# A two-stage attention and expert kernel: a greedy planner's order replaced by a written-out table of steps

## The chip, the cores and the metric

The kernel runs on one core of a Trainium2 chip. The metric is the device time of one execution in microseconds. The kernel before took 181.87 us in the median of three runs, which lay between 181.1 and 185.36 us.

## The reference

The input x has 4 batches of 10048 rows with 128 columns; `inducing` has 32 rows. The first part is attention in two steps, the second a mixture of 16 experts in 4 groups:

```python
def mab(q, kv):
    s = scale * (q @ kv.transpose(0, 2, 1))
    s = s - s.max(-1, keepdims=True)
    a = np.exp(s)
    a /= a.sum(-1, keepdims=True) + 1e-09
    return a @ kv
h = mab(I, x)            # 32 means of each batch
x2 = mab(x, h)           # each row: a mixture of its batch's 32 means
# mixture of experts, for each row of x2:
g_idx = np.argmax(x2 @ w_group); g_w = softmax(...)[g_idx]
e_idx = np.argmax(x2 @ w_expert[g_idx]); e_w = softmax(...)[e_idx]
out = g_w * e_w * (np.maximum(x2 @ w1[g_idx, e_idx], 0) @ w2[g_idx, e_idx])
```

Each row of x2 is a weighted sum of only 32 means. The fast path works out one expert for a batch from the sum of its means, checks afterwards that all its rows chose that expert and that no hidden unit changes its sign, and then needs the expert only for the means: a matrix G of 32 rows for each batch, so that a row of the output is its 32 attention weights times G. Where a check fails, a general path (behind a branch at the end) computes the batch again. With these inputs it isn't taken.

## The kernel before, in words

Each batch is cut into 5 chunks of 4 x 512 rows, named (b, k). x comes transposed, 1 MB a chunk, into a ring of ten tiles xk; for 11 of the 20 chunks the untransposed rows come too (xm, a ring of two), for the other 9 TensorE turns them (`turn`, L356, copied to xn).

First pass, `chunk`: scores of the 32 inducing rows (L392), their maxima on VectorE (L394 to L399), exp on ScalarE (L402, L405), TensorE turns the result (L410, copied to pt), and weighted sums of the rows are added up in hacc (L428, L434, L436). `common` (L443 to L459) brings the four row groups of a batch to one maximum and gives a factor fc. `mean` (L468 to L485) multiplies the sums of weights by fc, adds them over the four groups with a matmul against same_m (L471), inverts, scales hacc, and a second matmul (L482) gives hT, the means.

`routes` (L501 to L524): two matmuls of the means with the routing weights, then VectorE works out the index of the expert, pi (L505 to L517), and the routing rows own, rd and rbd (L520 to L524). `expert` reads pi into a register of SyncE (L531) and loads that expert's w1 and w2, 512 KB each (L532, L533). From these come G: L537, L547, L565, L575 on TensorE, with copies and VectorE steps in between.

Second pass, `att2`: scores against the means (L597), VectorE turns them (L602) and takes maxima (L606), GpSimd subtracts (L608), ScalarE takes exp (L610), the tile is turned (by TensorE, L644, or VectorE, L653), multiplied with the routing rows (L618), copied and turned again (L629). `gates` does a group of one to three chunks at once (L669 to L695) and gives a weight per row. `outputs`: GpSimd multiplies by it (L725), the tile is turned, four matmuls with G into two double PSUM banks (L743), two copies on ScalarE or VectorE, and the store of 1 MB (L749). All copies go through one helper, L323. `checks`, `bounds` and `verdict` prove the fast path.

All DMAs, loads and stores, are issued by SyncE, in order. So is every other engine's work: the helper `in_order` ties each instruction to the one before it on its engine.

What that order is comes from a planner at build time. Each of these functions is a generator that yields where it changes its engine. `Pace` follows the instructions written so far with a price for each kind and says when each engine and tile is free. `Plan.step` takes, among the jobs that may go on, those that start soonest, and of these the one with the least key (batch and chunk, with offsets such as LAG, and from 60 us on a list MOVES of single offsets). Loads are written when a tile of their ring is free (`load`). The helper `sooner` picks ScalarE or VectorE for a copy, `either` GpSimd or VectorE for a product. Where the planner sees TensorE idle for 0.75 us, `fill` writes matmuls of ones (L276) which nobody reads.

Of the kernel before, what the change touches and what calls it, by code (L numbers as in the profile page):

```python
# [8 lines left out]
F32 = mybir.dt.float32  # L9
# [36 lines left out]
BY_PE = {(B - 2, 0),(B-2, 1)} | {(B - 1, g) for g in range(3)}  # L46
TURNED = [(B - 1, NK - 1)]
FROM = 60.0
MOVES = {("att2", 0, 0): 0.97, ("att2", 0, 3): -1.54, ("att2", 0, 4): 0.83, ("att2", 1, 1): -1.59, ("att2", 1, 2): 0.72, ("att2", 2, 0): 2.99, ("att2", 2, 1): -1.6, ("att2", 3, 3): -0.39, ("checks", 0, 0): -0.44, ("checks", 0, 1): -0.21, ("checks", 1, 0): -1.76, ("checks", 2, 0): -0.25, ("checks", 2, 1): 1.39, ("checks", 3, 1): -0.16, ("chunk", 0, 0): -0.34, ("chunk", 0, 1): 2.5, ("chunk", 1, 3): -0.99, ("chunk", 2, 2): 1.06, ("chunk", 2, 3): 0.44, ("chunk", 3, 1): -0.47, ("chunk", 3, 2): -0.09, ("common", 0): 2.12, ("common", 2): 0.29, ("common", 3): -0.14, ("gates", 1, 0): -1.63, ("gates", 3, 0): -0.76, ("gates", 3, 2): 4.14, ("mean", 3): -3.64, ("outputs", 0, 0): -1.99, ("outputs", 0, 1): -1.63, ("outputs", 0, 3): 1.67, ("outputs", 1, 1): -0.98, ("outputs", 1, 2): -1.75, ("outputs", 2, 2): 1.19, ("outputs", 2, 3): 0.02, ("outputs", 3, 0): -1.03, ("outputs", 3, 4): -0.19, ("routes", 0): 1.12, ("turn", 0, 0, 0): 0.41, ("turn", 0, 0, 1): 1.96, ("turn", 0, 1, 1): -1.1, ("turn", 0, 3, 0): 0.09, ("turn", 2, 1, 0): -2.53, ("turn", 2, 3, 1): 0.09, ("turn", 3, 1, 0): 1.12, ("turn", 3, 3, 0): -1.91}
SIDES = {("at", 0, 0): 0, ("at", 0, 1): 1, ("at", 2, 1): 0, ("et", 0, 0): 0, ("et", 1, 2): 0, ("et", 3, 0): 0, ("out", 0, 4, 0): 0, ("out", 1, 0, 0): 0, ("out", 1, 1, 0): 0, ("out", 2, 1, 0): 0, ("out", 2, 2, 1): 0}  # L50
IDLE = 0.75
THIRD = 2.5
SECOND = -0.2
SWAP = 0.5
SPARE = 1.0
PAIRS = 2
LAG = 5

CHUNKS = [(b, k) for b in range(B) for k in range(NK)]
# [1166 lines left out]
```

## Time and profile before

| | |
|---|---|
| median of 3 runs | 181.87 us (181.1 to 185.36) |
| the profiled execution | 182.77 us, its span 180.9 us |
| mean granted TensorE clock | 0.983 |
| busy: PE, DVE, ACT, POOL | 158.7, 112.4, 111.7, 57.9 us |
| moved by DMA | 57.94 MB, 37.00 read from HBM, 20.58 written |
| expert loads issued, batches 0 to 3 | 37.7, 75.6, 113.8, 138.6 us |
| first and last store issued | 67.2, 173.8 us |

PE is TensorE, DVE VectorE, ACT ScalarE, POOL GpSimd, SP SyncE; PEld is TensorE's load of weights. A float32 matmul appears as two records of PE, a transpose as one. A group's line gives the source line, engine, operation, output and inputs, count, busy time in us and mean duration of one in ns, then the idle time of the engine just before, and what ended it. A line of the timeline or of the chain starts with the start in us and the duration in us; "x8" at its end is the number of records merged. Busy time is the union, so that records that overlap count once.

### The profile page before, as it was taken

The page shows a single profiled execution, that of the slowest core. Times are in us where ns is not written, and L with a number is a line of the kernel's source. Part 1 is how long each engine was busy: PE and PEld are TensorE (multiplying, and loading weights), DVE is VectorE, ACT ScalarE, POOL GpSimd, SP SyncE. Part 2 cuts the span into 40 slices and gives each one's busy share as a digit, 9 for nine tenths or more (in the row PEclk, how much of TensorE's full clock was granted, in tenths as well). Part 3 has the DMA queues.
Part 4 walks back from the last instruction along what each step waited for, and adds up shares of the span by engine and source line. Part 5 has one row for each costly group of instructions (what it writes and reads, how often), then busy time and mean ns, then how long its engine had stood idle before and what let it go on. Part 6 is the DMA issues. An engine that isn't in the chain of part 4 may idle for free.

```text
span 180.9 us, 4715 instructions
## 1 busy us (share of the span) xinstructions
PE 158.7 (88%) x1839; PEld 89.9 (50%) x1839; DVE 112.4 (62%) x334; ACT 111.7 (62%) x198; POOL 57.9 (32%) x85
## 2 busy tenths in 40 slices
PE   2998979998897999999989999989989889899910
PEld 1365746564573644543667446447753346456400
DVE  0143146479589882995897797775868856765300
ACT  3086744852467578558877399577448577756640
POOL 1000000024141943143217470152291934574000
PEclk9999999999999999999999999999999999999985
DMA  4999999999999578999999999895004996609791
GB/s 117 354 429 428 411 426 409 427 408 384 402 423 415 172 239 297 422 418 395 393 413 418 395 372 426 324 359 202 0 0 199 278 421 266 208 6 406 313 368 67
DMA packets 14524, 57.94 MB, mean 320 GB/s; under 512 B 1312, under 2 KB 7584, under 8 KB 8608
## 3 DMA queue, kind: packets, MB, share of 16 engines
q1 hardware_dynamic: 14496, 57.58, 81.9%
q8 instruction: 16, 0.26, 0.6%
q14 instruction: 12, 0.10, 0.1%
HBM read 37.00 MB, written 20.58 MB: 318 GB/s over the span
## 4 chain that ended last, share of the span: by engine, by line
PE 48%; DMA 32%; DVE 5%; ACT 5%; issue 3%; SPq 3%; ACTq 0%; DVEq 0%
DMA xk<-xT 16%; PE pp L743 10%; DMA xm<-xm 9%; PE ps L428 7%; DMA w1s<-w 7%; PE ps L597 5%; PE pp L356 4%; PE ps L392 4%; PE ps L644 4%; PE ps L276 3%; ACT osb L323 3%; PE ps L618 2%; PE ps L410 2%; PE ps L629 2%; PE ps L547 1%
## 5 line engine op out<-in xcount | busy, mean ns | idle before, releaser
L323 ACT COPY osb<-pp 128x1024 f32<-128x1024 f32 x40 | 39.1, 1020 | 18.7 <-PE pp L743 14.3
L608 POOL TENSOR_TENSOR e<-e,mxe 128x512 f32<-128x512 f32 x20 | 20.8, 1048 | 71.4 <-DVE mxe L606 70.3
L725 POOL TENSOR_TENSOR e<-e,w 128x512 f32<-128x512 f32 x20 | 20.6, 1048 | 26.4 <-ACT w L323 14.9
L743 PE MATMUL pp<-et,G 32*128 32x512 f32 x160 | 25.9, 640 | 0.1
L323 ACT COPY xn<-pp 128x1024 f32<-128x1024 f32 x18 | 18.1, 1018 | 9.0 <-PE pp L356 8.9
L394 DVE TENSOR_REDUCE mx<-ps 128x1 f32<-128x512 f32 (+1 forms) x20 | 13.5, 675 | 15.0 <-PE ps L392 14.7
L392 PE MATMUL ps<-xk,indT_sb 128*32 128x512 f32 (+1 forms) x144 | 18.6, 592 | 1.1 <-DMA xk<-xT 1.1
L597 PE MATMUL ps<-xk,hT 128*32 128x512 f32 x144 | 18.1, 598 | 0.6 <-ACT et L323 0.6
L602 DVE STREAM_TRANSPOSE e<-ps 128x512 f32<-128x512 f32 x20 | 14.0, 704 | 5.3 <-PE ps L597 4.3
L402 ACT ACTIVATE pe<-ps,nb 128x512 f32<-128x512 f32 (+1 forms) x20 | 13.8, 689 | 5.6 <-DVE nb L399 3.0
L323 ACT COPY pt<-ps 128x512 f32<-128x512 f32 (+2 forms) x24 | 11.8, 525 | 8.3 <-PE ps L410 8.1
L356 PE MATMUL pp<-cst,xk 128*128 128x128 f32 x128 | 16.5, 276 | 0.3 <-DMA xk<-xT 0.3
L356 PEld LDWEIGHTS pp<-cst,xk 128*128 128x128 f32 x128 | 14.0, 141 | 3.6 <-issue 1.4
L653 DVE STREAM_TRANSPOSE et<-e 128x512 f32<-128x512 f32 x21 | 14.2, 694 | 1.4 <-POOL e L725 1.4
L610 ACT ACTIVATE e<-e 128x512 f32<-128x512 f32 x20 | 12.3, 636 | 4.3 <-POOL e L608 4.3
L606 DVE TENSOR_REDUCE mxe<-e 128x16 f32<-128x512 f32 x20 | 13.5, 677 | 0.4
L743 PEld LDWEIGHTS pp<-et,G 32*128 32x128 f32 x160 | 7.9, 182 | 10.4 <-ACT osb L323 5.8
L428 PE MATMUL ps<-xm,pt 128*32 128x129 f32 (+1 forms) x352 | 11.9, 275 | 1.0 <-DVE hacc L436 0.5
L410 PE MATMUL ps<-cst,pe 128*128 128x128 f32 x80 | 12.4, 282 | 0.3 <-ACT w L323 0.3
L410 PEld LDWEIGHTS ps<-cst,pe 128*128 128x128 f32 x80 | 8.7, 142 | 5.4 <-ACT cr L405 1.6
L428 PEld LDWEIGHTS ps<-xm,pt 128*32 128x32 f32 (+1 forms) x352 | 9.3, 110 | 4.0 <-issue 1.7
L644 PE MATMUL ps<-cst,e 128*128 128x128 f32 x76 | 11.0, 280 | 0.0
(130 smaller groups left out, 229.1 us busy)
## 6 DMA issues: line engine op xcount, KB each, us to landing
xk<-xT SPq DMA_DIRECT2D x18, 1024.0 KB, 13.3
out<-osb SPq DMA_DIRECT2D x16, 1024.0 KB, 7.0
xm<-xm SPq DMA_DIRECT2D x11, 1032.0 KB, 12.4
out<-osb SPq DMA_DIRECT2D x3, 928.0 KB, 7.8
w1s<-w SPq DMA_DIRECT2D x4, 512.0 KB, 7.4
w2s<-w SPq DMA_DIRECT2D x4, 512.0 KB, 8.4
x<-xT SPq DMA_DIRECT2D x4, 256.0 KB, 3.8
x<-xT SPq DMA_DIRECT2D x1, 1024.0 KB, 8.4
```

The costliest lines, as they stand in the source:

```text
L323: (nc.scalar.copy if engine == ACT else nc.vector.tensor_copy)(out=out, in_=in_)
L356: nc.tensor.transpose(ps[:tw, (i * J + j) * P:(i * J + j + 1) * P], xks[b, k][:, j, at:at + tw], ident)
L392: nc.tensor.matmul(ps[32 * j:32 * j + 32, :w], lhsT=indT_sb, rhs=xks[b, k][:, j, off:], start=True, stop=True)
L410: nc.tensor.transpose(ps[:tw, t * P:(t + 1) * P], pe[:, t * P:t * P + tw], ident)
L428: nc.tensor.matmul(hq[32 * j:32 * j + 32, 0:C + 1], lhsT=pt[:tw, t, 32 * j:32 * j + 32], rhs=xn[:tw, t, j, :], start=(t == 0), stop=(t == ...
L597: nc.tensor.matmul(ps[32 * j:32 * j + 32, :], lhsT=hTs[b][:, 0:M], rhs=xks[b, k][:, j, :], start=True, stop=True)
L602: nc.vector.transpose(out=e.rearrange("p t m -> p (t m)"), in_=ps)
L608: either().tensor_tensor(out=e, in0=e, in1=mx[:, :, None].broadcast_to([P, TQ, M]), op=ALU.subtract)
L644: nc.tensor.transpose(ps[:, t * P:(t + 1) * P], e[:, t * J:(t + 1) * J, :].rearrange("p q m -> p (q m)"), ident)
L653: nc.vector.transpose(out=et, in_=e.rearrange("p t m -> p (t m)"))
L725: either().tensor_tensor(out=e, in0=e, in1=w[:, i * T:(i + 1) * T, None].broadcast_to([P, T, M]), op=ALU.mult)
L743: nc.tensor.matmul(pss[j // n][:, j % n * KW:(j % n + 1) * KW], lhsT=Gs[b][32 * j:32 * j + 32, :], rhs=rows, start=True, stop=True)
```

## The change

The planner goes: `Pace`, `Plan`, `Job`, the keys and offsets. In its place stands a table, ORDER, of 701 words. Each word is one step of one job: a letter for the kind, then batch and chunk (or group). The kernel goes through the words and lets the named generator run to its next yield. A second list, ON_DVE, names the copies and products that go to VectorE; all others go to ScalarE or GpSimd.

The letters: x, n loads; t turn; c chunk; h common; m mean; r routes; e expert; a att2; g gates; u outputs; k checks; q the ratios that were the end of `expert`; b bounds; v verdict; f a fill.

```python
for name in ORDER.split():
    job = (name[0], *map(int, name[1:]))
    if job not in jobs:
        jobs[job] = kinds[name[0]](*job[1:])
    next(jobs[job])
in_order(tc, begin)
```

The table begins, and goes on around the last batch's expert, and ends, with these words:

```
x01 f f f f f f f f f f f c00 t00 t00 t00 t00 f t01 c00 c00 c01 x02 c00 c00 x03 t01 t01 t01 x04 n02 c02 x10 n04 c01 c02 x11 x12 c00 c00 c03 c02 c02
...
m3 m3 e2 e2 a24 a24 u10 u21 u21 r3 r3 e3 e2 e2 u10 u10 u10 u10 a23 a24 g21 g21 a33 u20 u20 u20 u21 u21 u21 u21 a33 a33 a33 a33 r3 k21 a30 a30 a30 a30
a32 a32 a32 a32 g21 u20 u20 u22 u22 a33 a33 e3 a31 a31 a33 a33 a34 a30 u20 u22 a34 u20 a31 e3 e3 a32 a32 k21 u22 u23 u23 u23 a32 a32 a32 u24 e3 e3 u22
u23 u22 a32 a33 g31 q2 a31 a31 u23 u23 u23 a30 a30 u24 u24 a31 a31 e3 e3 g31 a30 u24 u24 e3 a31 a31 a30 a30 a31 u24 u24 u14 u14 u14 g31 u33 a34 a34
g30 g30 a34 e3 u14 u33 u33 f f u33 u33 u33 u33 g30 u32 u32 u32 q2 a34 a34 u32 u32 u32 u32 q0 u31 u31 u31 u30 u30 u30 a34 a34 a34 q3 q3 u31 u31 k30 k31
g32 g32 g32 u34 u34 k32 q1 q1 u31 u31 k32 f f u30 u30 u30 u30 f f f u34 u34 u34 u34 u34 q0 f f b b f f b b v f v v
```

Beside the order, the steps between a batch's last sum and its expert's loads are other ones. `common` sends the maximum to all groups with four matmuls and no copy, and multiplies fc into a copy of same_m; `mean` has one step of matmuls and one of VectorE:

```diff
-            nc.vector.tensor_tensor(out=ssum, in0=ssum, in1=fc, op=ALU.mult)
-            nc.tensor.matmul(tot_ps[:, 0:1], lhsT=same_m, rhs=ssum, start=True, stop=True)
-            nc.vector.tensor_scalar_add(rin, tot_ps[:, 0:1], EPS)
-            nc.vector.reciprocal(out=rin, in_=rin)
-            nc.vector.tensor_tensor(out=rin, in0=rin, in1=fc, op=ALU.mult)
-            nc.vector.tensor_scalar_mul(hqs, hacc[:, 0:C], rin)
-            nc.tensor.matmul(hT_ps[:, 0:P + 1], lhsT=hqs, rhs=same_m1, start=True, stop=True)
-            nc.vector.tensor_copy(out=hT4, in_=hT_ps[:, 0:P + 1])
...
+        nc.vector.tensor_scalar_mul(tl([P, P], f"samec{b % 2}"), same_m, fc)
...
+        nc.tensor.matmul(ps[:, P:P + M], lhsT=hacc[:, C:C + 1].broadcast_to([P, P]), rhs=sc[:, 0:M], start=True, stop=False)
+        nc.tensor.matmul(ps[:, P:P + M], lhsT=ones[0:1, 0:P], rhs=eps[:, 0:M], start=False, stop=True)
+        nc.tensor.matmul(ps[:, 0:P], lhsT=hacc[:, 0:C], rhs=sc, start=True, stop=True)
+        yield
+        nc.vector.reciprocal(out=rin, in_=ps[:, P:P + M])
+        nc.vector.tensor_tensor(out=hT4[:, 0:P].rearrange("p (j m) -> p j m", j=J), in0=ps[:, 0:P].rearrange("p (j m) -> p j m", j=J),
+                                in1=rin[:, None, :].broadcast_to([P, J, M]), op=ALU.mult)
+        nc.vector.reduce_sum(out=hT4[:, P:P + 1], in_=hT4[:, 0:M], axis=AX.X)
```

`routes` gives the index in one reduction, as a step of its own ahead of own, rd and rbd; the load of the register no longer checks its bounds:

```diff
-        nc.vector.tensor_reduce(out=pm, in_=at, axis=AX.X, op=ALU.min)
-        nc.vector.tensor_scalar(pi, pm[0:1, :], 40.0, float(E - 1), op0=ALU.add, op1=ALU.min)
+        nc.vector.reduce_max(out=pis[b], in_=at[0:1, :], axis=AX.X)
+        yield
+        nc.vector.reduce_max(out=pm, in_=at, axis=AX.X)
...
-        i = nc.sync.value_load(pi[0:1, 0:1], min_val=0, max_val=E - 1)
+        i = nc.values_load(pis[b][0:1, 0:1], engines=[SP], min_val=0, max_val=E - 1, skip_runtime_bounds_check_because="the greatest of 0 and numbers of experts")
```

A store is a step of `outputs`, with a word of its own in the table. The three VectorE steps that end `expert` become the job q. In the last batch, chunk 4 alone is stored in two halves, as before. A list of hints for the branch at the end also stands behind each store.

More of the change, by code (lines that the diff above doesn't have):

```diff
@@ L307, in fast @@
     sums = tl([P, NK, T], "sums")
-    todo = [(what, *c) for c in CHUNKS for what in ("x", "n") if what == "x" or c in LOADED][1:]
-    halves = {}
-    xks, xns, hTs, hsums, rbds, Gs, es, lgs, ws = {(0, 0): keep["x0"]}, {}, {}, {}, {}, {}, {}, {}, {}
-    def sooner(name=None):
-        if plan.late and name in SIDES:
-            return DVE if SIDES[name] else ACT
-        return ACT if pace.at.get(ACT, 0.0) <= max(pace.at.get(DVE, 0.0), pace.at.get(PE, 0.0)) + (0.0 if first.over else SPARE) else DVE
@@ L318, in either, with on_dve, copy @@
-    def either():
-        return nc.vector if first.over and pace.at.get(DVE, 0.0) + SWAP < pace.at.get(POOL, 0.0) else nc.gpsimd
-    def copy(engine, out, in_):
-        (nc.scalar.copy if engine == ACT else nc.vector.tensor_copy)(out=out, in_=in_)
+    xks, xns, hTs, hsums, rbds, Gs, es, lgs, ws, pis = {(0, 0): keep["x0"]}, {}, {}, {}, {}, {}, {}, {}, {}, {}
+    def on_dve(*name):
+        return "".join(map(str, name)) in ON_DVE
+    def copy(name, out, in_):
+        (nc.vector.tensor_copy if on_dve(*name) else nc.scalar.copy)(out=out, in_=in_)
@@ L340, in turn, with fill, load @@
-    def turn(b, k, h):
-        while (b, k) not in xks:
-            yield
-        yield PE, xks[b, k]
-        if (b, k) not in halves:
-            halves[b, k] = [(yield from xnring.take()), 0]
-        xn = halves[b, k][0]
+    def fill():
+        while True:
+            t = (banks.free[1] or banks.free[2])[0]
+            nc.tensor.matmul(t[:, 0:2 * P], lhsT=ones[:, 0:P], rhs=ones, start=True, stop=True)
+            yield
+    def load(what, b, k):
+        ring, src, have = (xring, xT, xks) if what == "x" else (xmring, xm, xns)
+        t = ring.take()
+        nc.sync.dma_start(out=t, in_=src[b, k])
+        have[b, k] = t
+        yield
@@ L348, in turn @@
+    def turn(b, k):
+        xn = xnring.take()
         off, w = fresh(k)
         n = TK // 2
[L350 to L359 removed]
@@ new lines, in common @@
+    def common(b):
+        nb = att1(b)[0][NK - 1]
+        ps = banks.take()
+        nc.tensor.transpose(ps[0:1, 0:P], nb, ident)
+        yield
+        row = tl([1, M], f"row{b % 2}")
+        nc.vector.tensor_reduce(out=row, in_=ps[0:1, 0:P].rearrange("o (j m) -> o m j", j=J), axis=AX.X, op=ALU.min)
+        banks.give(ps)
+        yield
+        ps = banks.take()
+        for j in range(J):
+            nc.tensor.matmul(ps[32 * j:32 * j + 32, 0:1], lhsT=row, rhs=ones[0:1, 0:1], start=True, stop=True)
+        yield
+        nba = tl([P, 1], f"nba{b}")
+        nc.vector.tensor_copy(out=nba, in_=ps[:, 0:1])
+        banks.give(ps)
+        yield
+        fc = tl([P, 1], f"fc{b}")
+        nc.scalar.activation(out=fc, in_=nb, func=AF.Exp, bias=nba, scale=-1.0)
+        yield
+        nc.vector.tensor_scalar_mul(tl([P, P], f"samec{b % 2}"), same_m, fc)
+        yield
@@ L584, in expert @@
         nc.vector.tensor_reduce(out=stats[:, 1, b:b + 1], in_=size, axis=AX.X, op=ALU.min)
-        bounded.append(b)
+        yield
     def att2(b, k):
-        while b not in hTs:
-            yield
-        yield PE, pace.loaded(keep["hT4"][b])
         if b == B - 1:
-            hint(ACT, DVE, POOL, nc.sync.engine)
-        ps = yield from banks.take()
+            hint(ACT, DVE, POOL, SP)
+        ps = banks.take()
         for j in range(J):
```

702 lines of the change are left out of this document (235 added, 467 removed).

## The prediction

> **What bounds the kernel now.** I read the page first, its share of busy time and its chain of work that ended last.
>
> ```profile
> span 180.9 us, 4715 instructions
> ...
> PE 158.7 (88%) x1839; PEld 89.9 (50%) x1839; DVE 112.4 (62%) x334; ACT 111.7 (62%) x198; POOL 57.9 (32%) x85
> ...
> PE 48%; DMA 32%; DVE 5%; ACT 5%; issue 3%; SPq 3%; ACTq 0%; DVEq 0%
> ```
>
> PE is busy 88% of the span and holds 48% of the chain. An average hides stages, so I next asked for busy time by stretch. I cut at 10 us (first loads in), at 60 us (the DMA share drops), at 138.57 us (the issue of the last batch's expert load) and at 173.72 us (the end of ACT's last copy).
>
> ```profile
> 10.00:60.00 50.00, 44.74 (x626) 28.29 (x626) 29.68 (x79) 29.43 (x58) 7.76 (x10) 1.00 1.01 413
> 60.00:138.57 78.57, 76.15 (x947) 42.41 (x950) 59.80 (x175) 55.12 (x103) 32.36 (x43) 1.00 0.78 300
> 138.57:173.72 35.15, 31.32 (x249) 16.21 (x246) 20.91 (x67) 24.96 (x36) 17.27 (x23) 1.00 0.75 286
> ```
>
> The columns are PE, PEld, DVE, ACT, POOL, clock, DMA share and GB/s. Before 138.57 us PE sits idle 5.26 + 2.42 us. Some busy time is only fill (L276, matmuls of ones whose result nobody reads):
>
> ```profile
> L743 PE MATMUL pp<-et,G 32*128 32x512 f32 x96 | 15.5, 640 | 0.1
> L597 PE MATMUL ps<-xk,hT 128*32 128x512 f32 x116 | 14.9, 598 | 0.0
> L644 PE MATMUL ps<-cst,e 128*128 128x128 f32 x32 | 4.9, 282 | 0.0
> L276 PE MATMUL pp<-ones 128*128 128x256 f32 x10 | 3.5, 456 | 1.2 <-DVE ones L1163 1.2
> L597 PE MATMUL ps<-x,hT 128*32 128x512 f32 x16 | 2.1, 598 | 0.0
> L276 PE MATMUL ps<-ones 128*128 128x256 f32 x2 | 0.6, 379 | 0.0
> ```
>
> These groups are those of PE up to 138.57 us. Of the 12 fill records two are the fill at the start; a fill is two records, and from the timeline
>
> ```profile
> 1.18 1.22 PE L276 MATMUL pp<-ones 128*128 128x256 f32 x2 [1.18 <-DVE ones L1163]
> 4.75 3.45 PE L392 MATMUL ps<-x,indT_sb 128*32 128x512 f32 x8 [2.36 <-DMA x<-xT]
> 8.13 1.97 PE L356 MATMUL pp<-cst,x 128*128 128x128 f32 x16
> 166.06 1.56 PE L276 MATMUL ps<-ones 128*128 128x256 f32 x6
> 169.20 0.70 PE L276 MATMUL ps<-ones 128*128 128x256 f32 x2
> ```
>
> a warm record costs (1.56 - 0.70) / 4 = 0.215 us. So 10 x 0.215 = 2.1 us of fill, and 9.8 us in all in which PE did nothing useful before the last expert load went out. Behind it, in the third stretch, PE idles only 3.8 us, but 26 of its records are fill; ACT is busy 24.96 of 35.15 us. What holds this stretch is the chain w1, expert, G, then five chunks of output.
>
> **The change, part by part.** All times below are of the profiled execution, 180.9 us of span and 182.77 us as a run; so 1.9 us lie around the span. The median of the three runs is 181.87, 0.9 us lower.
>
> **1. The order ahead of the last expert load.** A table has no time of its own; what it moves can be counted. I counted which PE steps stand ahead of `r3` and of `e3` in the text of the table, and in the groups above what had run by 138.57 us. Before: 96 records of L743 are the outputs of 12 chunks; of L597, 132 records less the four of the 24-record run that starts at 138.52, so 16 chunks; 32 of L644 are 8 turned tiles. After: the outputs of 8 chunks stand ahead of `r3`, one more (`u10`) runs while DVE works out the index; 15 chunks of `a`, a sixteenth partly; 6 turned tiles. Prices:
>
> ```profile
> 84.32 1.00 PE ps L597 x8
> ...
> 99.97 0.31 PE ps L452 x2
> ...
> 105.61 0.38 PE ps L471 x2
> ...
> 109.12 0.42 PE ps L482 x2
> ...
> 138.57 6.85 DMA w1s<-w
> ...
> 156.74 0.97 PE ps L644 x8
> ...
> 165.06 1.07 PE pp L743 x8
> ```
>
> That is 3 x 1.07 + 0.3 x 1.00 + 2 x 0.49 = 4.5 us of PE work moved behind the load. Against it, `common` has four small matmuls for one, and `mean` three for two. Four of L452's kind end somewhere between one (0.31) and four of them (1.24); I take 0.5. The mean's three go at 0.31 + 0.31 + 0.42 = 1.04 against 0.38 + 0.42. So (0.19 + 0.24) x 4 batches = 1.8 us more. Net: the load is 2.7 us earlier, between 1 and 4.5.
>
> **2. The hops from the mean to the load.** In the last batch:
>
> ```profile
> 130.61 0.34 DVE L436 SCALAR_TENSOR_TENSOR hacc<-hacc,cr,ps 128x129 f32<-128x129 f32 x1
> ...
> 135.25 0.40 PE L501 MATMUL ps<-wr_sb,hT 128*128 128x20 f32 x2
> ...
> 137.31 0.36 SPq L749 DMA_DIRECT2D out<-osb  x1
> 137.32 0.14 DVE L517 TENSOR_SCALAR pi<-pm 1x1 int32<-1x1 f32 x1
> ...
> 138.57 0.35 SPq L532 DMA_DIRECT2D w1s<-w  x1
> ```
>
> From hacc's end (130.95) to w1's issue takes 7.6 us: 4.3 to the first matmul of `routes`, 2.2 to pi, 1.1 to the issue. The change takes one PE hop out (L471) with the DVE steps L468, L474, L476, L477 and L479; fc is multiplied into same_m ahead of the chain. It leaves three DVE steps on 128 columns or fewer (about 0.9 us by L436's 0.34 and smaller) and one matmul group (1.04). With about 0.2 us per handover I get 2.4 for 4.3 us, and some 0.4 less on the pi side, as `own` no longer lies between pi and SP. So the hops are about 2.3 us shorter per batch, between 1 and 3.5. This is not added to the sum: while that chain ran, PE idled or filled (four fills and 0.7 us idle lie between 128 and 132 us), and that time is among the 9.8 us. For batches 0 and 1 the table uses none of it: `e0` and `e1` come well behind `r0` and `r1`.
>
> **3. Idle and fill ahead of the load.** The table has one fill between the head and `u33`. Its PE order puts `c`, `a` or `u` steps where PE waited for hacc, w1 or nb. How much of the 9.8 us comes back no row can show; the ends are none and all of it. I take 6, as the named waits (fill 2.1, the last chain, waits for w1 and nb) are the better part of it.
>
> **4. Eleven fills at the head.** Before, one fill, then PE waits for x0; the first eight L392 took until 8.20. Eleven fills from 1.18 us cost 0.43 each warm, and 0.43 x 1.22 / 0.70 = 0.75 cold (the first pair against a warm pair). All warm, they end at 5.9, inside the wait for x0, and cost nothing. All cold, they end at 9.9, and the first chunk, at 1.07 x 1.74, at 11.8: 3.6 late. L392 at 8 in 3.45 us was slow or waiting, and L356 at 8.13 was at its later speed after some 3.4 us of work, so I take four cold and seven warm: 7.7 + 1.07 = 8.7, **0.5 us late**. [...]
>
> Loads: x01 to x04, n02, x10, n04 are issued without waiting for anyone, as before. At 413 GB/s a 1 MB load takes 2.54 us; the seventh is due near 8 + 7 x 2.54 = 25.8 us, its use in the table stands behind some 19 us of PE work, near 27.7. The cover is 1.4 to 2 us at each of them; gone, it would cost that much once.
>
> So w1 of the last batch goes out at 138.57 - 2.7 - 6.0 + 0.5 = **130.4 us** (124.3 at best, 141.2 at worst). Its landing keeps 6.85 us: `u13`'s store still stands just ahead on SP as the store at 137.31 does now; `u10`'s and eleven more now stand behind. PE has 8.7 us of steps between `r3` and the use of w1, the load 2.3 + 6.85 after `r3`, so at most 0.5 us of waiting, inside the next term.
>
> **5. Behind the load ACT sets the pace.** ACT's groups from the issue on:
>
> ```profile
> L323 ACT COPY osb<-pp 128x1024 f32<-128x1024 f32 x18 | 17.7, 1016 | 9.5 <-PE pp L743 6.7 <-issue 1.1 <-ACT et L323 1.0
> L323 ACT COPY et<-ps 128x512 f32<-128x512 f32 x7 | 3.9, 595 | 1.0 <-PE ps L644 1.0
> L610 ACT ACTIVATE e<-e 128x512 f32<-128x512 f32 x5 | 3.0, 641 | 0.0
> L674 ACT ACTIVATE ex<-x 128x192 f32<-128x192 f32 (+1 forms) x3 | 1.1, 353 | 0.0
> L323 ACT COPY lt<-ps 128x128 f32<-128x128 f32 x2 | 0.5, 266 | 0.2
> L323 ACT COPY G<-ps 128x128 f32<-128x128 f32 x1 | 0.3, 270 | 0.0
> ```
>
> Durations add up to 27.5 us, their union is 24.96, a factor of 0.907. Behind `e3` the table has 23 output copies on ACT (12 chunks, one half on DVE), 8 turned tiles, 5 exps, 4 of the gates, one lt, G and mT: 23.4 + 4.8 + 3.2 + 1.4 + 0.3 + 0.6 = 33.7, times 0.907 = 30.6 us. ACT idled 10.2 us there, 6.7 of it waiting for L743. With three more chunks of outputs ready to fill that, I take half, 5.1: **35.7 us**, from 30.6 up to 30.6 / 0.71 = 43.1 at today's share. DMA is close: 12 chunks and the weights, 13.3 MB, at 413 GB/s are 32 us, still under it.
>
> **6. The tail.**
>
> ```profile
> 170.72 3.41 SPq L749 DMA_DIRECT2D out<-osb  x3
> ...
> 171.80 1.93 ACT L323 COPY osb<-pp 128x1024 f32<-128x1024 f32 x2 [1.10 <-issue]
> ```
>
> From ACT's end (173.72) to the end are 7.2 us: the last store and the close. `b` and `v` now stand behind the last chunk on PE and DVE. Some ten short steps with fills, about 4.6 us, run beside the two copies and the store; cost 0, up to 2 if the branch waits for them.
>
> Sum: 130.4 + 35.7 + 7.2 = 173.3 us of span, 175.2 as that run, less 0.9 against the median: **174.3 us**.
>
> **The rivals.**
> (a) *The waits come back under other names.* Only 3 us of the 9.8 are recovered and ACT idles 9: 133.4 + 39.6 + 7.2 = 180.2, at the median 181.2. For it: a fixed order that meets real durations stalls where the old one did, in order on each engine. Against: the old stalls stand in few places, around the chain.
> (b) *ACT becomes the bound behind the load, and the kernel is slower.* Three more chunks of output lie there. ACT's share has been as low as
>
> ```profile
> 150.00:160.00 10.00, 9.13 (x98) 5.51 (x98) 7.29 (x30) 6.65 (x14) 4.32 (x6) 1.00 0.54 205
> ```
>
> 0.665. At that share 30.6 / 0.665 = 46.0, and with 4.5 us recovered 131.9 + 46.0 + 7.2 = 185.1, at the median 186.1. It decides below a share of about 0.68.
> (c) *All of it works*: 124.3 + 30.6 / 0.93 + 7.2 = 164.4, at the median 165.4; ACT would have to run at 93%.
> (d) *The head is all cold*: 3.1 over my sum, 177.4; this lies in the forecast's own range.
> (e) *PE cools down in a stall.* With hardly a fill until `u33`, a stall of 4 us could slow what follows as the first eight L392 were slow: 3.45 us for what takes 1.00 later (L597, the same shape), so up to 2.4 on top. In each of three places that is 174.3 + 19.2 = 193.5. Against it, PE's longest wait from 10 us on is
>
> ```profile
> 25.10 0.27 PE L443 MATMUL ps<-cst,nb 128*1 128x128 f32 x1 [1.07 <-DVE nb L399]
> ```
>
> 1.07 us. [...]
> (f) The change doesn't shorten the load: then 6.85 us stay, as I have it already.
>
> **How the numbers follow.** A measurement of this kernel can tell about 2% from no change: below 178.2 is faster, above 185.5 slower. Forecast with (d) 0.53 (170 to 178), (c) 0.09: faster 0.62. (a) 0.23: same. (b) 0.13 and (e) 0.02: slower 0.15. The range leaves out most of (c) and most of (b) and (e): 168 to 184; the forecast's own is 170 to 178.
>
> **What would show it.** The last w1 is issued near 130 us, with 9 chunks of L743 ahead of it. PE idle and fill between 10 us and that point add up to about 4 us. From hacc to that issue take about 5.3 us. ACT is about 86% busy from there to its last copy. The first chunk's L392 end near 8.7. The prediction is wrong if the load goes out after 136 us, or if ACT's share behind it is under 0.7.

## The result, and the profile after

The changed kernel takes 173.96 us (median of four runs, 173.28 to 174.35) beside 182.19 us of the kernel before (median of four, 181.1 to 185.36). The ratio is 0.956, with a 95% interval from 0.950 to 0.962. Ratios, here and below, leave out executions that lie over 1.5% above the fastest of their kernel (here the one of 185.36 us); medians and ranges take all. The forecast was 174.3 us. The profiled execution took 174.04 us, its span 172.3, where the sum of the prediction had 173.3. That the two agree so well is partly luck: three of its terms were off by 4.5, 1.6 and 1.9 us, and the errors nearly cancel.

From the page of the changed kernel, the same three lines as of the kernel before:

```profile
span 172.3 us, 4811 instructions
...
PE 159.7 (93%) x1881; PEld 94.2 (55%) x1881; DVE 116.5 (68%) x328; ACT 109.2 (63%) x192; POOL 57.4 (33%) x85
...
PE 83%; DMA 5%; ACT 3%; DVE 3%; issue 1%; ACTq 0%
```

PE's busy time has hardly changed (158.7 before), but it now holds 83% of the chain instead of 48%, and DMA 5% instead of 32%. Most of what PE waited for before has gone, and PE is what is left; 7% of the chain are fills (L183).

Busy time by stretch, cut at the issue of the last expert load (now 125.87 us) and at the end of ACT's last copy (163.15 us); the columns are PE, PEld, DVE, ACT, POOL, clock, DMA share and GB/s:

```profile
10.00:60.00 50.00, 49.40 (x704) 32.63 (x703) 34.30 (x88) 30.74 (x60) 7.48 (x9) 1.00 1.02 415
60.00:125.87 65.87, 64.48 (x872) 36.21 (x870) 53.09 (x143) 47.71 (x91) 31.44 (x39) 1.00 0.86 323
...
125.87:163.15 37.28, 35.85 (x275) 18.30 (x271) 26.57 (x79) 29.30 (x41) 17.64 (x25) 1.00 0.86 332
```

Ahead of the load PE idles 0.60 + 1.39 us, where it idled 5.26 + 2.42 before. Behind it ACT is busy 29.30 of 37.28 us, a share of 0.786.

The groups of PE up to the load that tell what stands ahead of it (line, engine, operation, tiles, count, busy us, mean ns):

```profile
L419 PE MATMUL ps<-xk,hT 128*32 128x512 f32 x112 | 14.0, 597 | 0.2 <-DVE hT L311 0.2
L550 PE MATMUL pp<-et,G 32*128 32x512 f32 x72 | 10.4, 640 | 0.0
L461 PE MATMUL ps<-cst,e 128*128 128x128 f32 x24 | 3.9, 285 | 0.0
L419 PE MATMUL ps<-x,hT 128*32 128x512 f32 x16 | 2.1, 599 | 0.0
```

These are the outputs of nine chunks (72 records), 16 chunks of `att2` (128) and 6 turned tiles (24), as counted from the table.

The chain from the last batch's hacc to the load, from the timeline:

```profile
119.10 0.30 DVE L274 SCALAR_TENSOR_TENSOR hacc<-hacc,cr,ps 128x129 f32<-128x129 f32 x1
...
120.42 0.41 PE L305 MATMUL ps<-samec,hacc 128*128 128x32 f32 x2
...
122.80 0.30 PE L323 MATMUL ps<-wr_sb,hT 128*128 128x20 f32 x2
...
124.56 0.16 DVE L337 TENSOR_REDUCE pi<-pat 1x1 int32<-1x16 f32 x1
...
125.87 0.35 SPq L354 DMA_DIRECT2D w1s<-w  x1
```

From hacc's end (119.40) it is 6.5 us, against 7.6 before: 3.4 to the first matmul of `routes` instead of 4.3, 1.9 to pi instead of 2.2, and 1.15 from pi to the issue as before.

And the end. The branch to the general path, on PE, in the changed kernel (L937) and in the kernel before (L1175); the columns are count, shortest, median and longest duration in ns, and the first and last start in us:

```profile
L937 PEldq EVENT_SEMAPHORE  x2: 51/51/51, 170.3 to 170.5; - x2
...
L937 PEldq COMPARE_BRANCH  x1: 4417/4417/4417, 165.9 to 165.9; - x1
L937 DVEq COMPARE_BRANCH  x1: 84/84/84, 165.9 to 165.9; - x1
```

```profile
L1175 SPq EVENT_SEMAPHORE  x9: 17/17/17, 178.7 to 179.6; - x9
...
L1175 PEldq COMPARE_BRANCH  x1: 1257/1257/1257, 171.6 to 171.6; - x1
```

Before, SP's waits for the last stores ended latest (179.6 us, then 1.3 us of close). Now PE stands at its branch for 4.42 us, from 165.87 to 170.28, and the end comes 1.97 us behind that. The other engines pass the same branch in 65 to 84 ns.

### The profile page after: what moved, and what is told of

It is laid out like the page before. It is cut to its first block, busy times and chain, and to the rows that moved or that the text cites. A ratio compares the mean times of both kernels' runs of the same rounds, so it can differ in the third digit from the quotient of the medians.

```text
span 172.3 us, 4811 instructions
## 1 busy us (share of the span) xinstructions
PE 159.7 (93%) x1881; PEld 94.2 (55%) x1881; DVE 116.5 (68%) x328; ACT 109.2 (63%) x192; POOL 57.4 (33%) x85
## 4 chain that ended last, share of the span: by engine, by line
PE 83%; DMA 5%; ACT 3%; DVE 3%; issue 1%; ACTq 0%
PE pp L550 13%; PE pp L206 10%; PE ps L419 10%; PE ps L235 9%; PE ps L267 9%; PE ps L183 7%; PE ps L253 6%; DMA xk<-xT 5%; PE ps L461 5%; PE ps L437 3%; PE ps L447 2%; ACT osb L169 1%; PE ps L368 1%; PE ps L387 1%; PE ps L307 1%
## 5 line engine op out<-in xcount | busy, mean ns | idle before, releaser
L169 ACT COPY osb<-pp 128x1024 f32<-128x1024 f32 x39 | 38.3, 1016 | 14.9 <-PE pp L550 9.8
L538 POOL TENSOR_TENSOR e<-e,w 128x512 f32<-128x512 f32 x19 | 19.7, 1051 | 17.5 <-DVE w L497 10.5
L169 ACT COPY xn<-pp 128x1024 f32<-128x1024 f32 x17 | 16.9, 1017 | 12.2 <-PE pp L206 12.2
L235 PE MATMUL ps<-xk,indT_sb 128*32 128x512 f32 (+1 forms) x144 | 18.5, 592 | 0.0
L206 PE MATMUL pp<-cst,xk 128*128 128x128 f32 x128 | 16.5, 275 | 0.6 <-DMA xk<-xT 0.6
L183 PE MATMUL ps<-ones 128*128 128x256 f32 x48 | 14.6, 452 | 1.2 <-DVE ones L925 1.2
L206 PEld LDWEIGHTS pp<-cst,xk 128*128 128x128 f32 x128 | 14.1, 141 | 1.9 <-DMA xk<-xT 0.8
L431 ACT ACTIVATE e<-e 128x512 f32<-128x512 f32 x20 | 12.8, 640 | 3.1 <-POOL e L429 2.9
L468 DVE STREAM_TRANSPOSE et<-e 128x512 f32<-128x512 f32 x21 | 14.2, 692 | 0.1
L169 ACT COPY pt<-ps 128x512 f32<-128x512 f32 (+2 forms) x21 | 10.6, 524 | 4.8 <-PE ps L253 3.4
L183 PEld LDWEIGHTS ps<-ones 128*128 128x128 f32 x48 | 10.3, 228 | 5.1 <-issue 2.3
```

The costliest lines, as they stand in the source:

```text
L169: (nc.vector.tensor_copy if on_dve(*name) else nc.scalar.copy)(out=out, in_=in_)
L183: nc.tensor.matmul(t[:, 0:2 * P], lhsT=ones[:, 0:P], rhs=ones, start=True, stop=True)
L206: nc.tensor.transpose(ps[:tw, (i * J + j) * P:(i * J + j + 1) * P], xks[b, k][:, j, at:at + tw], ident)
L235: nc.tensor.matmul(ps[32 * j:32 * j + 32, :w], lhsT=indT_sb, rhs=xks[b, k][:, j, off:], start=True, stop=True)
L468: nc.vector.transpose(out=et, in_=e.rearrange("p t m -> p (t m)"))
L538: either("u", b, k).tensor_tensor(out=e, in0=e, in1=w[:, i * T:(i + 1) * T, None].broadcast_to([P, T, M]), op=ALU.mult)
```

## The experiments

My theory after the result: the load's issue sets when the last stretch begins; it came earlier because PE's waits went, through the order and the hops together; behind it ACT sets the pace; and the end waits for PE's branch. The rivals: the hops alone or the order alone bring the gain; the load is hidden; PE, DMA or the output buffers hold the last stretch; the last stores hold the end. Ratios below are to the kernel before, measured beside it on the same chip, with 95% intervals; the changed kernel's is 0.956.

### Order and hops

**e1: the hops alone, with the planner.** In the kernel before, `common`, `mean` and `routes` are those of the changed kernel; the planner chooses the order as ever.

```diff
-            nc.tensor.matmul(all_ps[:, 0:1], lhsT=row4.rearrange("o j m -> o (j m)"), rhs=ones[0:1, 0:1], start=True, stop=True)
+            for j in range(J):
+                nc.tensor.matmul(all_ps[32 * j:32 * j + 32, 0:1], lhsT=row, rhs=ones[0:1, 0:1], start=True, stop=True)
...
-        plan.add(mean(prev), key(b, NK) - 0.6, DVE, name=("mean", b))
+        plan.add(mean(prev), key(b, NK) - 0.6, PE, name=("mean", b))
```

> The kernel before with its own planner, and only the new hops: four small matmuls in place of the copied row, fc multiplied into same_m, the mean in one step of PE and one of DVE, pi by one maximum. Theory (the fixed order brings the gain, the hops only clear the way for it): the last w1 goes out 1 to 2.3 us earlier than the 138.6 us of before, hacc to w1 takes about 6.5 us instead of 7.6, and the time is 1 to 2 us under the 182 of before (ratio 0.99 to 0.995); the planner will also shift other steps, which adds about 1 us of uncertainty to either side. Rival (the hops bring the gain): at least 5 of the 8 us, a ratio of 0.97 or less.

Measured: 188.05 us (186.87 to 190.54), ratio 1.030 (1.020 to 1.040): slower, with the lower end of the interval just at 2%. Both theories missed. Timeline around the last batch's chain:

```profile
131.32 0.28 DVE L448 TENSOR_REDUCE row<-ps 1x32 f32<-1x128 f32 x1 [0.43 <-PE ps L445]
...
134.36 0.24 PE L453 MATMUL ps<-ones,row 1*32 1x1 f32 x8
...
135.76 0.35 DVE L438 SCALAR_TENSOR_TENSOR hacc<-hacc,cr,ps 128x129 f32<-128x129 f32 x1 [0.86 <-PE ps L430]
...
144.38 0.35 SPq L528 DMA_DIRECT2D w1s<-w  x1
```

The planner now puts 2.8 us of other work between the row (ready at 131.60) and its matmuls, and hacc itself is 5.2 us later than before (136.11 against 130.95). The load goes out at 144.38. Its offsets had been set for other steps, so this run says that the planner's order does not carry over, and little of the hops themselves.

**e5: the hops alone, in the old order.** To take the planner out, I wrote its own sequence of steps down word by word, each word one step of one job, so that PE's instructions stand in the same order as in the kernel before, and then put the new hops in. `replay` goes through these words.

```diff
-    while plan.jobs:
-        plan.step()
+    plan.replay()
```

> The kernel before with its own order of steps written down word by word (its planner no longer chooses; PE's instructions are the same ones in the same order), and then only the hops replaced by the new ones: the new mean on PE stands where same_m x ssum stood, the rest of the old chain falls away. Theory (hops and order need each other, since the run with the long hops in the new table lost 6 of the 8 us): each load goes out 0.5 to 2.5 us earlier than before, the last near 136 instead of 138.6, ratio 0.98 to 0.995. Rival 1 (hops alone bring most): ratio 0.97 or less. Rival 2 (in the old order the hops are worth nothing, since the steps around them stand where the long chain needed them): ratio 0.995 to 1.01.

Measured: 185.29 us (184.16 to 189.28), ratio 1.012 (1.001 to 1.023): no gain, and rather a small loss, which even rival 2 did not have. A part of the reason is in the timeline:

```profile
133.04 0.34 DVE L454 SCALAR_TENSOR_TENSOR hacc<-hacc,cr,ps 128x129 f32<-128x129 f32 x1
...
136.39 0.19 DVE L496 TENSOR_REDUCE hT<-hT 128x1 f32<-128x32 f32 x1
...
138.29 0.40 PE L511 MATMUL ps<-wr_sb,hT 128*128 128x20 f32 x2
...
141.32 0.35 SPq L542 DMA_DIRECT2D w1s<-w  x1
```

The means are there at 136.58, but PE reaches `routes` only at 138.29, since the steps that once covered the long chain still stand ahead of it. From hacc's end to `routes` it is 4.9 us, 0.6 more than in the kernel before. That is the smaller part: the load goes out 2.75 us later than before, and hacc itself ends 2.4 us later (133.38 against 130.95). The delay builds up over the batches (their loads go out 0.3, 1.6, 1.9 and 2.75 us later than before), and its largest step, 1.3 us between the first two loads, holds a stretch of 3.4 us at half the granted clock (59.6 to 63.0 us, shown in the last section). So the loss isn't the price of the hops alone.

**e2: the new table with the long hops.** `mean` is the old one, in four words instead of two; the added words stand between the steps that the table has there anyway. `common` has its copied row again. `routes` stays the short one, so only a part of the hops is undone.

```diff
+        nc.vector.tensor_tensor(out=ssum, in0=ssum, in1=fc, op=ALU.mult)
+        yield
+        nc.tensor.matmul(ps[:, 0:1], lhsT=same_m, rhs=ssum, start=True, stop=True)
...
+        nc.tensor.matmul(ps[:, 0:P + 1], lhsT=hqs, rhs=same_m1, start=True, stop=True)
+        yield
+        nc.vector.tensor_copy(out=hT4, in_=ps[:, 0:P + 1])
```

> The changed kernel's table with the long mean of before: DVE ssum*fc, PE same_m, DVE rin and hqs, PE hqs x same_m1, DVE copy of hT (two PE hops instead of one), and the row copied for one matmul in common; the added words stand between the filler steps that the table already has there, and the choice of the expert stays as in the changed kernel. Theory (order first): hacc of the last batch to w1 takes 7 to 7.6 us instead of 6.5, the load goes out about 1 us later, near 127, less 1 us of PE work saved by the cheaper matmuls; the time is 0 to 2 us over the changed kernel's 174 (ratio to before 0.955 to 0.97). Rival (the hops bring the gain): 178 or more.

Measured: 180.06 us (179.76 to 181.92), ratio 0.989 (0.981 to 0.998). The rival's side: without the short hops the table loses 6 of the 8 us. What PE waited for from 10 us to the load (at 132.69), in total, times, and longest:

```profile
PE ps L313 <- DVE hacc L310: 2.4, 2, 1.6
PE ps L295 <- DVE rowj L293: 2.3, 2, 1.4
PE ps L323 <- DVE hqs L320: 0.7, 1, 0.7
```

The added steps on DVE stand in DVE's queue behind other work, and PE stands behind them. All waits of this list add up to 7.8 us against 1.9 in the changed kernel, and one stretch ran at half the granted clock besides:

```profile
88.00:95.00 7.00, 4.03 (x65) 2.96 (x67) 4.87 (x11) 3.02 (x6) 2.63 (x3) 0.99 0.99 377
95.00:98.00 3.00, 3.00 (x26) 1.22 (x26) 1.88 (x5) 1.34 (x2) 1.28 (x2) 0.50 0.69 283
```

The load is 6.8 us later than in the changed kernel, and the span 5.8 us longer. So the four cases are:

| | long hops | short hops |
|---|---|---|
| old order | 1 | 1.012 (e5), 1.030 replanned (e1) |
| new table | 0.989 (e2) | 0.956 |

Neither part alone brings 2%, as these runs have it; together they bring 4.4%. Two limits. e2 and e5 put steps by hand into an order that had been set for others, so they price the parts in these orders and not in the best order for them. And both hold one stretch of 3.4 us at half the granted clock amid their work, which neither the kernel before nor the changed one has: at most 1.7 us each, 0.9%, as an estimate from that length. Without it e2 would come near 0.980 and e5 near 1.003, still far from 0.956.

### Does the load set the end?

**e4: two stores ahead of the last load.** The first word of `e3` moves behind the last word of `u21`.

```diff
-m3 m3 e2 e2 a24 a24 u10 u21 u21 r3 r3 e3 e2 e2 u10 u10 u10 u10 a23 a24 g21 g21 a33 u20 u20 u20 u21 u21 u21 u21 a33
+m3 m3 e2 e2 a24 a24 u10 u21 u21 r3 r3 e2 e2 u10 u10 u10 u10 a23 a24 g21 g21 a33 u20 u20 u20 u21 u21 u21 u21 e3 a33
```

> The changed kernel, with the first word of e3 (the last expert load) moved behind the last word of u21 in the table: on SP the stores of two chunks are then issued ahead of w1 and w2, as stores stood ahead of the load in the kernel before. Theory (the issue of this load sets when the last stretch begins): w1 goes out near 130 instead of 125.9, lands after 6 to 7.5 us instead of 5.3, PE waits for it for 2 to 5 us, and the time is 3 to 6 us over the changed kernel's 174. Rival (PE has enough other work, the load is hidden): within 1 us of 174.

Measured: 180.18 us (179.44 to 182.2), ratio 0.985 (0.981 to 0.989), 6.2 us over the changed kernel's median: the theory, and a little more than its range. w1 went out at 130.85, 5.0 us later. PE's waits behind it, and the stretch after the longest of them:

```profile
PE ps L365 <- DMA w1s<-w: 4.5, 1, 4.5
```

```profile
136.00:139.00 3.00, 2.47 (x16) 0.91 (x20) 0.00 (x0) 0.90 (x2) 0.11 (x1) 0.51 1.10 406
```

ACT's last copy ends at 169.26, that is 38.4 us behind the load, against 37.3 in the changed kernel. In e2 it is 169.97 - 132.69 = 37.3 again. So the last stretch has about the same length in these three runs. That a later load costs time is shown by e4. That the load is what holds the changed kernel isn't: there w1 lands 4.6 us after its issue, at 130.5, PE first reads it at 131.87, and no wait for it is among PE's. In e2 PE does not wait for it either. So the issue marks how far the whole order has come, with 1.4 us to spare, and e4 pushed it past that.

### What holds the last stretch?

**e7: five output copies from ACT to DVE.** `o301 o311 o321 o331 o341` are added to ON_DVE.

> The changed kernel with the second half of the last five chunks' output copies on DVE instead of ACT (five copies of 1.02 us; DVE has 11 us free in that stretch). Theory of the prediction (ACT sets the pace behind the last load): the stretch from the last w1 to the last output copy shrinks from 37.3 by 2 to 5 us, time 169 to 172. Rival (PE and the chain through it hold this stretch; PE was busy 36.7 of 38.1 us there): stretch within 1 us of 37.3, time 173 to 175; DVE's chain to the verdict may become later.

Measured: 182.48 us (180.97 to 184.73), ratio 0.999 (0.994 to 1.004): the whole gain lost, as neither side expected. In the profiled execution, 2 us slower than the median, PE's longest wait was for a copy that DVE had taken over:

```profile
PE pp L550 <- DVE osb L169: 2.7, 1, 2.7
```

The copies stand in DVE's order where the words put them, in front of the gates and turned tiles of the last chunks. Behind the waits the clock fell, twice, for some 13 us in all; one of these stretches:

```profile
165.00:170.00 5.00, 5.00 (x14) 2.49 (x15) 1.50 (x4) 0.00 (x0) 0.00 (x0) 0.50 0.71 283
```

All ten executions have a mean granted clock of 0.949 to 0.969, against 0.984 to 0.991 of the changed kernel, so this is not of the profiled one alone. Half of the 13 us, by estimate the most that the clock can have cost, would be most of the 8.5 us lost. The run is a test of DVE's order and of the clock and not of ACT's pace, so it decides nothing on the question.

**e9: shorter copies on ACT.** The queues stay as they are; only the copies of the last batch shrink.

```diff
+            m = n // 2 if b == B - 1 else n
-                copy(("o", b, k, h), osb[:, n * h:n * h + n], ps.rearrange("p (j n) -> p j n", n=KW))
+                copy(("o", b, k, h), osb[:, n * h:n * h + m], ps.rearrange("p (j n) -> p j n", n=KW)[:, 0:m])
```

> The changed kernel, but in the last batch each output copy takes half its columns (512 of 1024); the stores still move whole tiles, so half of the last batch's output is not computed. Nine copies on ACT and none of PE's work become shorter: about 10 x 0.4 = 4 us less for ACT behind the expert chain. Theory of the prediction (ACT sets the pace behind the last load): last w1 to last copy shrinks from 37.3 by 2.5 to 4.5 us, time 169.5 to 171.5. Rival (the chain through PE, DVE and the gates sets it, and the landing of stores): it shrinks by less than 1.5 us, time 172.5 to 174.2.

Measured: 171.98 us (171.57 to 172.25), ratio 0.941 (0.936 to 0.947). From the last w1 to the last copy:

```profile
125.86:160.87 35.01, 33.66 (x271) 17.53 (x268) 25.94 (x76) 24.97 (x41) 17.63 (x25) 1.00 0.88 344
```

ACT's work fell by 4.3 us (29.30 to 24.97), the stretch by 2.3 (37.28 to 35.01). That lies between the two. Of the 2.3 us, 0.9 are the last two copies themselves (1.07 us for 1.93); the other 1.4 came earlier, as the last chunk's matmuls start at 158.58 and not 160.01. So ACT holds about half of that stretch's end. What holds the rest no run here isolates: PE is busy 33.66 of the 35.01 us, but 4.94 of these are fills.

**e10: half the stores of the last batch.**

```diff
+            if b == B - 1:
+                js = slice(js.start, (js.start + js.stop) // 2)
```

> The changed kernel, but the last batch's stores move only the first half of each tile (2.5 MB less, 6 us of DMA at 413 GB/s); half of the last batch's output is not written. In the trace of the changed kernel ACT waits up to 1.9 us for a store that holds its output buffer, and stores issued at 147.65 and 150.88 land about 7 us later. Theory (DMA holds the last stretch through these buffers): last w1 to last copy shrinks by 1 to 3 us, and PE's branch, fetched beside fewer stores, takes under 2.5 us instead of 4.4: time 168.5 to 171. Rival (DMA is hidden): stretch within 0.5 us; only the branch becomes shorter, time 171.5 to 174.

Measured: 172.77 us (172.12 to 173.69), ratio 0.944 (0.939 to 0.950): the rival in the stretch, and not in the branch. The stretch, and PE's branch:

```profile
126.10:163.38 37.28, 35.85 (x275) 18.28 (x271) 26.60 (x79) 29.32 (x41) 17.67 (x25) 1.00 0.72 278
```

```profile
L939 PEldq COMPARE_BRANCH  x1: 4294/4294/4294, 165.7 to 165.7; - x1
```

To the hundredth the same 37.28 us: DMA is hidden there. And in this execution PE's branch is nearly as long as in the changed kernel (4.29 us), although the DMA had been far less busy ahead of it (share 0.38):

```profile
156.00:163.20 7.20, 7.12 (x34) 3.53 (x32) 4.06 (x18) 5.40 (x7) 1.63 (x3) 1.00 0.38 147
```

So stores that fill the DMA are not needed for a slow branch, as I had thought. This execution was the slowest of the four, though (173.69 us). The median lies 1.2 us under the changed kernel's; whether the branch was shorter in the others no profile shows, so that gain stays open.

**e11: other output buffers.** The last batch takes its output tiles from the ring of x tiles, idle by then.

```diff
-        osb = oring.take()
+        spare = xring if b == B - 1 and xring.tiles else oring
+        osb = spare.take()
```

> The changed kernel, whose last batch takes the output tiles from the ring of x tiles, which is idle by then, instead of the ring of three osb tiles: no output copy waits for an earlier store any more. Theory (the wait for a store's landing costs ACT its 1.36 us ahead of the copy at 155.2 and what follows): last copy 0.7 to 1.5 us earlier, time 0.5 to 1.5 us under 174. Rival (PE's matmuls are late anyway, by the chain of the last gates): less than 0.4 us.

Measured: 174.64 us (172.87 to 175.05), ratio 0.954 (0.947 to 0.961): nothing gained, the rival. The copy at 155.7 us, on which I had read "issue 1.36" in the changed kernel (there at 155.3), now says what it waits for:

```profile
155.73 1.01 ACT L169 COPY xk<-pp 128x1024 f32<-128x1024 f32 x1 [1.32 <-PE pp L550]
```

That it was late by PE's matmuls in the changed kernel too is my reading; it fits e10, where the stores are half as long and the stretch is the same.

### Fills and the clock

**e6: one fill at the head instead of eleven.** Ten words `f` behind `x01` go.

> The changed kernel with one fill at the head instead of eleven. In its trace the eleven fills (22 records) ran from 1.18 to 8.67 us and the first eight records of L235 ended at 9.66, against 8.20 in the kernel before, so they were 1.5 us late and not the 0.5 of the prediction. Theory (the fills delay the first chunk and warm nothing that matters): first chunk ends near 8.2, last w1 0.5 to 1.5 us earlier, time 0.5 to 1.5 us under 174. Rival (without them the first steps run as slowly as the 3.45 us of the first L392 in the kernel before, and the loads are late anyway): within 0.5 us of 174 or up to 1 us slower.

Measured: 173.48 us (172.49 to 174.33), ratio 0.951 (0.942 to 0.960); not told apart from the changed kernel, the rival. PE's first steps here, and in the changed kernel (L241 is its L235, L212 its L206):

```profile
4.74 3.97 PE L241 MATMUL ps<-x,indT_sb 128*32 128x512 f32 x8 [2.34 <-DMA x<-xT]
8.64 2.94 PE L212 MATMUL pp<-cst,x 128*128 128x128 f32 x16
...
11.84 1.04 PE L212 MATMUL pp<-cst,xk 128*128 128x128 f32 x8
```

```profile
1.18 7.49 PE L183 MATMUL ps<-ones 128*128 128x256 f32 x22 [1.18 <-DVE ones L925]
8.60 1.07 PE L235 MATMUL ps<-x,indT_sb 128*32 128x512 f32 x8
9.59 1.97 PE L206 MATMUL pp<-cst,x 128*128 128x128 f32 x16
...
11.83 1.05 PE L206 MATMUL pp<-cst,xk 128*128 128x128 f32 x8
```

Without the fills the first chunk starts 3.9 us earlier and takes 3.97 us instead of 1.07, and the 16 transposes 2.94 instead of 1.97. From 11.8 us on the two are the same within 0.02 us: what the fills delay, the faster steps behind them make up. It is not a load that hides the delay, since the next step's x (01) lands at 10.9 us (11.0 in e6) and PE reads it at 11.83. Nor is all of the 3.97 us a slow PE: its weight loads waited 1.5 us for x, whose first chunk comes in four loads, while the matmul records took 1.06 us each instead of 0.60. The last w1 goes out at 125.70 against 125.87.

**e8: no fills at the end.** The last twelve words `f` go.

> The changed kernel without the last twelve fills (between u33 and the verdict); the twelve at the head stay. In the trace of the changed kernel three fills stand ahead of the last chunk's outputs on PE while its tile is ready, and more ahead of b. Theory (they hold the last chunk back): last output copy 0.7 to 1.5 us earlier, time 0.7 to 1.5 us under 174. Rival (PE slows down in the gaps without them, as the first steps of the head are slow): L550 records longer than 0.64 us on average in the last ten us, time 0 to 2 us over 174.

Measured: 174.17 us (173.77 to 174.92), ratio 0.955 (0.948 to 0.963): no gain. The last chunk's matmuls did start 0.5 us earlier (159.52 for 160.01), but ran at half the granted clock, 2.68 us instead of 1.14. These two stretches, and the same stretch of the changed kernel:

```profile
156.10:159.50 3.40, 2.21 (x8) 0.61 (x9) 2.39 (x8) 3.13 (x5) 1.62 (x3) 1.00 0.56 231
159.50:164.00 4.50, 3.57 (x11) 1.60 (x11) 1.83 (x12) 2.49 (x3) 0.00 (x0) 0.50 0.99 405
```

```profile
159.00:164.00 5.00, 5.00 (x26) 2.95 (x25) 2.25 (x16) 2.62 (x3) 0.00 (x0) 1.00 0.98 390
```

Both sides of the expectation were right at once: the fills delay the last chunk, and they keep the clock up for it.

### The end

**e3: an earlier hint for PE's branch.** The hint in `verdict` stays; one more stands in each output chunk of the last batch.

```diff
+        if b == B - 1:
+            hint(PE)
         pss = [banks.take(n) for _ in range(J // n)]
```

> The changed kernel with one more branch hint for PE in each output chunk of the last batch, so the last five stand up to some 18 us before the branch; the hint in the verdict stays. Theory (the end waits for PE's branch, which took 4.42 us because its hint came 2.75 us before it while stores filled the DMA): PE's branch takes under 1.3 us, the span from ACT's last copy to the end shrinks from 9.15 to 6.5 to 7.5 us, and the time falls by 1.5 to 2.5 us to about 172. Rival (the last store or the close holds the end anyway): less than 0.5 us gained.

Measured: 172.58 us (172.02 to 172.82), ratio 0.945 (0.939 to 0.951). PE's branch:

```profile
L939 SPq EVENT_SEMAPHORE  x9: 17/17/17, 166.3 to 168.1; - x9
...
L939 PEldq COMPARE_BRANCH  x1: 497/497/497, 165.7 to 165.7; - x1
```

0.50 us instead of 4.42. From ACT's last copy (163.02) to the end (170.56) it is 7.5 us instead of 9.1, and SP's waits for the last stores, which end at 168.1, are again the latest thing ahead of the close. The theory's side, with 1.4 us gained where it had 1.5 to 2.5.

**e12: the hint and the spare buffers together.**

> The early branch hint for PE (172.6 us when run alone) and the spare output buffers together, as a candidate for a kernel that beats both. If the buffers gain 0.5 to 1.5 us and the gains add, 171 to 172.2 us; if the buffers gain nothing, 172.3 to 172.8.

Measured: 172.9 us (172.36 to 173.58, six runs), ratio 0.946 (0.942 to 0.951). The branch is short again (0.50 us), the buffers add nothing. So the version that beats both kernels is the changed kernel with the early hint, e3, by about 1.4 us; it was not timed beside the changed kernel itself, but both traces show where it comes from: 170.56 us of span for 172.25, with everything up to ACT's last copy the same within 0.15 us.

## Why the prediction was right, and where it was not

**1. The order.** The counts held: nine chunks of outputs, 16 of `att2` and 6 turned tiles ahead of the load. The price was too low. I took 1.07 us for a chunk's outputs, from a run of 8 records that stood alone. Over the whole stretch before, 96 records cost 15.5 us, 1.29 a chunk; after, 72 cost 10.4, 1.16 a chunk. So this item alone is 5.1 us and not 3.2. The matmuls that the hops add were priced too high: 1.3 us more than before over the four batches and not 1.8 (and (0.19 + 0.24) x 4 is 1.7), as the four small ones of `common` take 0.95 us in all where the single one took 1.51. With 0.3 us of `att2` and 1.1 of turned tiles, both about as predicted, that makes 5.2 us. By the times of the load PE's work ahead of it is smaller by 12.7 - 7.4 = 5.3 us, where I had 2.7 less 0.5 for the head. The 12.7 us are 138.57 - 125.87, the 7.4 are those of point 3.

**2. The hops.** Predicted 5.3 us in the last batch, measured 6.5: the piece from hacc to `routes` is 3.4 and not 2.4, as PE has other steps ahead of the mean's matmuls (hacc ends at 119.40, they start at 120.42), and the piece from pi to the issue did not shrink. The 0.2 us per handover was an estimate: in this chain of the kernel before, the gap from the end of a step to the start of the next on another engine is 0.04 us three times (L459 to L468, L471 to L474, L482 to L485), 0.06 once (L468 to L471) and 0.26 once (L479 to L482). The larger mistake is that I gave the hops no price in the sum, since the waits that they end were already counted. In the count that is right, but it hid that those waits come back with the long hops: e2 shows 5.8 us of the span. That was rival (a) with a definite cause.

**3. Idle and fill.** 9.8 us before. After, 0.60 + 1.39 us of idle and the one fill near 11.4 us (0.43), 2.4 in all: 7.4 recovered and not 6. The load was due at 130.4 and went out at 125.87. The step that failed is thus two terms of the sum, the price of PE's work (2.6 us too small, or 3.1 with the head) and the waits recovered (1.4 too small).

**4. The head.** The first chunk ends at 9.66 us, later than the 8.7 predicted, for the fills ran from 1.18 to 8.67. But the delay costs nothing, since without the fills the first steps are slower by as much (e6), so the 0.5 us in the sum should have been 0. The first fills cost more than the warm price, as allowed for: 7.49 us for 22 records, 0.34 each, against 0.215. That four of the eleven would be slow was an estimate, and no run shows it: up to 6.00 us the trace has 11 records in 4.82 us, 0.44 each, and from there 12, one of them in both stretches, in 2.67 us, about 0.23 each.

**5. Behind the load.** Predicted 35.7 us at an ACT share of 0.857, measured 37.3 at 0.786. ACT's work was nearly as counted (29.3 for 30.6), its idle time was 8.0 and not 5.1. "ACT sets the pace" is half right: with 4.3 us less of its work the stretch shrank by 2.3 (e9). What holds the rest is open: PE is busy 35.85 of 37.28 us there, but 5.79 of these are fills. That DMA is under it held (e10). The load landed in 4.6 us and not 6.85, and PE did not wait for it.

**6. The tail.** Predicted 7.2 us, "up to 2 if the branch waits for them"; measured 9.1. The ends were right and the value was not. The steps of `b` and `v` do end before the stores (164.96), but PE's hint stands with them, 2.75 us ahead of the branch, and the branch then takes 4.42 us. Before, the hint came 3.46 us ahead and the last store covered it. The step that I did not cost is the hint, which moved with `v`.

**The rivals.** (a) did not happen in the changed kernel; e2 is what it looks like. (b) would have needed an ACT share under 0.68. (c) was nearly true of the load (125.87 against its 124.3) and not of what follows it. (d) did not happen: the head ends at 9.66 and not 11.8. (e), to which I gave 0.02, did happen in other runs: PE was granted half the clock (0.50 or 0.51) for a stretch in e2, e4, e5, e7 and e8. The stall of 4 us in it was an estimate, and no run shows that it takes one: ahead of the stretch stands a wait of 4.5 us in e4, and none over 0.40 us in e5. Its price was misread: the 3.45 us of the first eight L392 are in part waits for x, 1.5 us of them, as in e6. In the changed kernel no wait of PE between 10 and 165 us is longer than 0.6 us, and at the end, where e8 without the fills has a clock of 0.50 (159.5 to 164 us), it has 1.00 (159 to 164 us).

## What to carry to other kernels

Price moved work by the group's busy time over its whole stretch, not by one run that stands alone: the difference was 1.9 us, more than a third of what the order took off PE ahead of the load. A shorter chain and an order are one change: the short hops cost time in the old order and the table gained only 1% with the long ones, so neither can be judged with the other left as it was. When the last steps of a kernel move, look at what else moves with them, hints for a branch included.

## What the runs showed of the hardware

**A branch whose hint came late held up its engine.** PE's branch took 4417 ns with its hint 2.75 us ahead, 1257 ns with the hint 3.46 us ahead (the kernel before), and 497 ns with the first hint 21 us ahead (e3). The other traces bear it out: with the hint 2.4 to 2.9 us ahead it took 3.4 to 4.4 us (e2, e4, e6, e8, e9, e10, e11), with 3.4 to 3.5 us ahead 2.1 (e1) and 0.50 us (e5). The hint's row in the changed kernel:

```profile
L982 PEldq BRANCH_PREFETCH_HINT  x1: 45/45/45, 163.1 to 163.1; - x1
```

From the hint to the end of the branch it was 4.0 us in e5, 4.7 before, 7.2 in the changed kernel, 6.7 with half the stores (e10). The DMA's load alone does not set it: from 156.0 to 163.2 us its share was 0.38 in e10 and 0.81 in the changed kernel. While PE stood at the branch in the changed kernel, from 165.87 to 170.28 us, five packets (49 KB) went through the profile's two queues of instructions; in the kernel before, from 171.57 to 172.83 us, none did. What they carry no row says, so what sets the time stays open; what the rows show is the price of a late hint, 4417 ns where an early one left 497.

**The clock fell without a long wait.** In e5 the stretch from 59.6 to 63.0 us was granted half the clock (0.50), though no wait of PE in the 3.4 us ahead, a stretch as long, was longer than 0.40 us; PE had been busy 2.09 of these 3.4 us:

```profile
56.20:59.60 3.40, 2.09 (x40) 1.04 (x31) 3.02 (x9) 1.75 (x7) 1.32 (x2) 1.00 0.98 400
59.60:63.00 3.40, 3.40 (x40) 2.87 (x40) 1.18 (x2) 1.75 (x3) 3.12 (x5) 0.50 0.23 96
```

e8 is alike (2.21 of 3.4 us busy and no wait over 1.14 us, then a clock of 0.50), and in e4 a single wait of 4.5 us stood ahead of a clock of 0.51. In the kernel before, a stretch of that length with 2.69 us busy, fills among it, lost nothing:

```profile
128.80:132.20 3.40, 2.69 (x15) 1.92 (x15) 2.56 (x7) 1.53 (x4) 2.39 (x3) 1.00 0.00 0
```

The busy share of one such stretch does not decide it alone, either. This one of e2, with less than e5's, kept the full clock (1.00); only behind the next one (91.5 to 94.9 us, 1.84 of 3.4 us busy) did it fall, to 0.50 from 95 to 98 us:

```profile
88.10:91.50 3.40, 1.99 (x18) 1.25 (x20) 1.90 (x5) 2.50 (x5) 0.74 (x1) 1.00 0.96 349
```

In e5 four short waits within 3.4 us, 1.3 us in all, were enough. What sets the clock no row here shows.
